# The output product of a mixture kernel as one fp32r product over 96 rows, with the combine weights turned in the last block

## The chip, the cores and the metric

The kernel runs on one core of a Trainium2 chip. The metric is device time in microseconds of one execution; three executions of the kernel before took 632.43, 634.65 and 635.01, median 634.65.

## The reference, cut to what matters

Chunked attention gives x (3072 tokens x 512). A rational feed-forward network follows, and then a soft mixture of 8 experts with 4 slots each, 32 slots in all:

```python
# x: 3072 x 512 from attention
h = x @ w_in                       # 512 x 2048
g = P(h) / (Q(h) + 1e-6)           # a cubic over a quadratic, by element
x = g @ w_out                      # 2048 x 512
logits = x @ phi                   # 3072 x 32
d = softmax(logits, over tokens)   # dispatch
slot_input = d.T @ x               # 32 x 512
for e in range(8):                 # 4 slots per expert
    slot_out[e] = relu(slot_input[e] @ w1[e]) @ w2[e]   # 512x1024, 1024x512
c = softmax(logits, over slots)    # combine
out = c @ slot_out                 # 3072 x 32 times 32 x 512
```

## The kernel before, in words

Tokens are worked in six blocks of 512. A block has eight steps; a step makes 256 hidden features h (24 fp32r products per step, L309: high and low parts of both operands), evaluates the rational function on ScalarE, VectorE and GpSimd, adds to the logits (L326) and turns the result to token order (L334, evicted by L335). The order is written by hand in `KN`: attention of the next block is sliced between the steps; the last block has none and uses `KN['ordl']`. `run_step` issues one part of a step; step kk makes the h of step kk + 1 and finishes the element work of step kk - 1.

After a block, in steps 1 and 2 of the next one, `soft1`, `soft2` and `soft3` work on its logits. `soft2` makes the combine weights `ce`, unnormalised: 128 token rows x 4 x 32 slots. `soft3` adds the dispatched tokens (L387), and ends with a turn of `ce` (L396) into `c_all`, where four groups of 32 partitions hold the 32 slots of four token groups.

Behind the loop: the sums are multiplied by w_out (L605), spread to the experts (L613, L617), then by w1 (L625, in two halves `eq` of four experts), passed through relu, turned (L642) and multiplied by w2 (L652). The result is summed over its four partition groups by a product with `stack` (L658) and evicted (L660). The output stage is the loop at the end: per block two halves, each two products of 32 rows (L668), one VectorE and one ScalarE eviction that scale by the normaliser (L675, L673), and one store (L676). The half tile comes from a pool of two buffers.

w_out, w1 and w2 make 8 + 32 + 32 loads of 512 KB. `fill` issues them on SyncE in a fixed order (`wants`) into whatever slots come free: each call names a pool and a count, and SyncE waits there until the slot's last reader is done. Which slots are named, and where, is the prefetch plan. The first calls stand at step `last` (40), two more `win` slots follow in each step of the last block, and the rest stand between the products behind the loop.

Of the kernel before, what the change touches and what calls it, by code (L numbers as in the profile page):

```python
# [10 lines left out]
F32 = mybir.dt.float32  # L11
F32R = mybir.dt.float32r
AF = mybir.ActivationFunctionType
ALU = mybir.AluOpType
# [27 lines left out]
def tile_chunk_attention__rational__soft_moe(  # L42
# [15 lines left out]
    PE, ACT, DVE, POOL, SP = nc.tensor, nc.scalar, nc.vector, nc.gpsimd, nc.sync  # L58

    NPAIR, P, HP, _ = qw.shape  # L60
    NMEM, D = 8, vwin.shape[-1]
    S = 768
    NT, DM = out.shape
    DFF = 2048
    NSLOT = phi.shape[1]
# [4 lines left out]
    BLK = 512  # L70
    NBLK = NT // BLK
    TT = BLK // P
# [14 lines left out]
    const = Pool(ctx.enter_context(tc.tile_pool(name="const", bufs=1)))  # L87
# [3 lines left out]
    p_S = Pool(ctx.enter_context(tc.tile_pool(name="p_S", bufs=5)))  # L91
    p_g = Pool(ctx.enter_context(tc.tile_pool(name="p_g", bufs=4)))
    p_q = Pool(ctx.enter_context(tc.tile_pool(name="p_q", bufs=1)))
    p_k = Pool(ctx.enter_context(tc.tile_pool(name="p_k", bufs=1)))
    p_v = Pool(ctx.enter_context(tc.tile_pool(name="p_v", bufs=1)))
    p_a4 = Pool(ctx.enter_context(tc.tile_pool(name="p_a4", bufs=2)))
    p_s2 = Pool(ctx.enter_context(tc.tile_pool(name="p_s2", bufs=1)))
    p_dr = Pool(ctx.enter_context(tc.tile_pool(name="p_dr", bufs=1, space=bass.MemoryType.DRAM)))
    p_sm = Pool(ctx.enter_context(tc.tile_pool(name="p_sm", bufs=1)))
# [4 lines left out]
    def bank(shape):  # L104
        return ps_m("m", shape)
# [4 lines left out]
    ident = const("ident", [P, P])  # L110
# [4 lines left out]
    phi_sb = u_acc[:, 0:NC * NSLOT].rearrange("p (c s) -> p c s", c=NC)  # L115
    csum = const("csum", [P, NTILE])
    run = const("run", [P, 4])
    c_all = const("call", [P, NBLK, P])

    ahead = {}  # L120

# [111 lines left out]
    def attention_block(b):  # L233
        new_xt(b)
        for n in range(BLK // (2 * P)):
            yield from attention(b * BLK // (2 * P) + n)
# [77 lines left out]
    st = {}  # L314
# [51 lines left out]
    def soft2(b):  # L366
        pl = st.pop("pl")
        pb = bank([P, TT, 64])
        for tt in range(TT):
            PE.transpose(pb[:, tt, :], pl[0:64, tt * P:tt * P + P], ident[0:64, 0:64])  # L370
        p_tok = p_sm("ptok", [P, TT, NSLOT])
        ACT.activation(p_tok, pb[:, :, 0:32], AF.Copy)  # L372
        cm = p_sm("cm", [P, TT])
        ce = p_sm("ce", [P, TT, NSLOT])
        DVE.tensor_reduce(cm, pb[:, :, 32:64], AX.X, ALU.max)
        DVE.tensor_tensor(ce, pb[:, :, 32:64], cm.unsqueeze(2).to_broadcast([P, TT, NSLOT]), ALU.subtract)
        ACT.activation(ce, ce, AF.Exp)
        DVE.tensor_reduce(csum[:, b * TT:b * TT + TT], ce, AX.X, ALU.add)
        st["ptok"], st["ce"] = p_tok, ce

    def soft3(b):
        ce = st.pop("ce")
        p_tok = st.pop("ptok")
        pb = bank([P, BLK])
        for tt in range(TT):
            for j in range(4):
                PE.matmul(pb[32 * j:32 * j + 32, :], lhsT=p_tok[:, tt, :], rhs=gts[b, j][:, tt, :],  # L387
                          start=(tt == 0), stop=(tt == TT - 1))
        if b == 0:
            DVE.tensor_copy(u_acc, pb)  # L390
        else:
            DVE.scalar_tensor_tensor(u_acc, u_acc, alpha, pb, ALU.mult, ALU.add)
        for j in range(4):
            del gts[b, j]
        pb = bank([P, P])
        PE.transpose(pb, ce.rearrange("p t s -> p (t s)"), ident)  # L396
        ACT.activation(c_all[:, b, :], pb, AF.Copy)

    def wp_chunk(i):
        t = wo.pop(i)  # L400
# [51 lines left out]
    total = NBLK * NSTEP  # L452
# [21 lines left out]
    def fill(pool, tag, count, views):  # L474
        for _ in range(count):
            t = pool(tag, [P, views * 1024])
            for m in range(views):
                if not wants:
                    return
                want = wants.pop()  # L480
                dst = t[:, 1024 * m:1024 * m + 1024]
                if want[0] == "1":
                    src = w1[want[1], want[2] * P:want[2] * P + P, :]
                else:
                    dst = dst.rearrange("p (j d) -> p j d", j=2)
                    src = wo_dr[want[1]] if want[0] == "o" else w2[want[1], want[2]]
                SP.dma_start(out=dst, in_=src)
                got[want] = dst

    def w_out_rows(ft):  # L490
        return got["o", ft // 2][:, ft % 2, :]

    last = total - NSTEP
# [75 lines left out]
    for kk in range(total + 4):  # L569
        b, i = divmod(kk, NSTEP)  # L570
        if kk == last:
            fill(p_q, "q", 1, 1)
            fill(p_a4, "a4", 2, 1)
            fill(p_k, "k", 1, 2)
            fill(p_v, "v", 1, 2)
            fill(p_xt, "xt", 2, 2)
        if i == 0 and b < NBLK - 1:
            state["att"] = attention_block(b + 1)
        for what in KN["ord0" if b == 0 else "ord" if b < NBLK - 1 else "ordl"]:
            run_step(kk, what)  # L580
        if last <= kk < total:
            fill(p_win, "win", 2, 1)
        if kk == total - 1:
            fill(p_xt, "xt", 2, 2)
        if kk == total + 2:
            fill(p_T, "T", 5, 1)
            fill(p_S, "S", 5, 1)
# [8 lines left out]
    pb = bank([P, 4, P])  # L596
# [4 lines left out]
    pb = bank([P, DM])  # L601
    for n in range(4):
        for j in range(4):
            ft = 4 * j + n
            PE.matmul(pb[32 * j:32 * j + 32, :], lhsT=ut[:, n, 32 * j:32 * j + 32],  # L605
                      rhs=w_out_rows(ft),
                      start=(n == 0), stop=(n == 3))
    fill(p_v, "v", 1, 2)
    si = p_s2("s2", [P, DM])
    ACT.activation(si, pb, AF.Copy, scale=rden)  # L610
    pb = bank([P, NC, NSLOT])
# [3 lines left out]
    POOL.memset(sz, 0.0)  # L615
    for e in range(NE):
        DVE.tensor_copy(sz[:, :, e, 4 * e:4 * e + 4], pb[:, :, 4 * e:4 * e + 4])  # L617
    hts = []
    for eq in range(2):
        hb = ps_h("h", [P, 2, 512])  # L620
        for c in range(NC):
            for hh in range(2):
                for j in range(4):
                    e = 4 * eq + j
                    PE.matmul(hb[32 * j:32 * j + 32, hh, :], lhsT=sz[:, c, e, :],  # L625
                              rhs=got[("1", e, c)][:, 512 * hh:512 * hh + 512], start=(c == 0), stop=(c == NC - 1))
        if eq == 0:
            fill(p_win, "win", 12, 1)
        else:
            fill(p_win, "win", 4, 1)  # L630
            fill(p_T, "T", 5, 1)
        h1 = p_a4("a4", [P, 2, 512])
        for hh in range(2):
            if hh:
                ACT.activation(h1[:, hh, :], hb[:, hh, :], AF.Relu)
            else:
                DVE.tensor_scalar(h1[:, hh, :], hb[:, hh, :], 0.0, None, ALU.max)
        hT = (p_k if eq else p_q)("k" if eq else "q", [P, 8, P])
        for hh in range(2):
            pb = bank([P, 4, P])  # L640
            for n in range(4):
                PE.transpose(pb[:, n, :], h1[:, hh, n * P:n * P + P], ident)  # L642
            if hh:
                ACT.activation(hT[:, 4:8, :], pb, AF.Copy)
            else:
                DVE.tensor_copy(hT[:, 0:4, :], pb)
        hts.append(hT)
    so = ps_l("lg", [P, DM])
    for eq in range(2):
        for n in range(8):  # L650
            for j in range(4):
                PE.matmul(so[32 * j:32 * j + 32, :], lhsT=hts[eq][:, n, 32 * j:32 * j + 32],  # L652
                          rhs=got[("2", 4 * eq + j, n // 2)][:, n % 2, :],
                          start=(eq == 0 and n == 0), stop=(eq == 1 and n == 7))
    sos = p_s2("s2", [P, DM])
    ACT.activation(sos, so, AF.Copy)
    pb = bank([P, DM])
    PE.matmul(pb, lhsT=stack, rhs=sos, start=True, stop=True)  # L658
    so4 = p_s2("s2", [P, DM])
    ACT.activation(so4, pb, AF.Copy)  # L660
    rows = out.rearrange("(b r t) d -> b r t d", r=P, t=TT)
    for b in range(NBLK):
        ob = p_xt("xt", [P, TT, DM])
        for half in range(2):
            pb = ps_h("h", [P, 2, DM])
            for m in range(2):
                g = 32 * (2 * half + m)
                PE.matmul(pb[:, m, :], lhsT=c_all[g:g + 32, b, :], rhs=so4[g:g + 32, :], start=True, stop=True)  # L668
            for m in range(2):
                tt = 2 * half + m  # L670
                cs = csum[:, TT * b + tt:TT * b + tt + 1]
                if m:
                    ACT.activation(ob[:, tt, :], pb[:, m, :], AF.Copy, scale=cs)  # L673
                else:
                    DVE.tensor_scalar(ob[:, tt, :], pb[:, m, :], cs, None, ALU.mult)  # L675
            SP.dma_start(out=rows[b, :, 2 * half:2 * half + 2, :], in_=ob[:, 2 * half:2 * half + 2, :])  # L676
# [60 lines left out]
```

## Time and profile before

| what | us |
|---|---|
| median of three executions | 634.65 |
| profiled execution | 633.84 |
| its span | 632.1 |
| TensorE busy | 561.1 |
| VectorE busy | 461.8 |
| ScalarE busy | 421.4 |
| GpSimd busy | 123.5 |

The span is what the trace covers; the profiled execution's own time lies a little over it. Busy shares are means over stages with different limits, so the end of each stage is read from the chain of waits.

### The profile page before, as it was taken

Reading aid. Unit: us, or ns where it says so; the run is one execution under the profiler, and the core shown is the slowest. Engines: PE = TensorE matmul, PEld = TensorE weight load, DVE = VectorE, ACT = ScalarE, POOL = GpSimd, SP = SyncE. Lnnn points to the kernel's source line nnn. Section 1 sums busy time; section 2 is a strip of 40 time slices with the busy share of each in tenths; the row PEclk is TensorE's granted clock in tenths of the full one; section 3 lists DMA queues with packets and bytes.
Section 4 is the critical chain, followed back from the end, with each engine's and each line's share of the span. In section 5 each row is a group of like instructions: output and inputs, shape, how many; then the busy total and the mean of one; then the engine's idle time right before and its main releaser. Section 6 shows DMA issues by size and latency. Waiting matters only on the chain.

```text
span 632.1 us, 13355 instructions
## 1 busy us (share of the span) xinstructions
PE 561.1 (89%) x5784; PEld 377.0 (60%) x5784; DVE 461.8 (73%) x578; ACT 421.4 (67%) x542; POOL 123.5 (20%) x74
## 2 busy tenths in 40 slices
PE   1349999999999999999999999999999997489965
PEld 1338886767666776667765667656776574235211
DVE  3775799977997869978699786997877957620022
ACT  2576899988775878758777586776869688310022
POOL 0121122321231312313133131322223322000000
PEclk9999999999999999999999999999999999689985
DMA  7996745320212202121022210321175236779936
GB/s 308 414 369 218 314 150 200 108 94 1 102 69 90 78 2 101 68 102 67 3 100 68 99 50 21 101 68 63 53 270 184 70 131 226 298 282 409 405 143 266
DMA packets 21754, 97.39 MB, mean 154 GB/s; under 512 B 3136, under 2 KB 3136, under 8 KB 16704
## 3 DMA queue, kind: packets, MB, share of 16 engines
q1 hardware_dynamic: 18000, 79.70, 33.6%
q0 software_dynamic: 2880, 16.78, 7.2%
q8 instruction: 45, 0.74, 0.5%
q10 hardware_dynamic: 816, 0.07, 0.1%
q14 instruction: 13, 0.11, 0.1%
HBM read 86.05 MB, written 10.49 MB: 153 GB/s over the span
## 4 chain that ended last, share of the span: by engine, by line
PE 56%; DVE 18%; ACT 12%; issue 6%; DMA 6%; POOL 1%; DVEq 0%; POOLq 0%; ACTq 0%; SPq 0%
PE h L309 28%; PE lg L326 6%; PE m L334 5%; PE m L387 4%; DMA g<-in_moe_w_in_dram 3%; DVE T L540 3%; DVE T L541 2%; DVE T L555 2%; PE h L625 2%; ACT S L528 2%; ACT g L335 2%; DVE S L529 2%; ACT T L530 2%; DVE T L556 2%; PE h L668 2%
## 5 line engine op out<-in xcount | busy, mean ns | idle before, releaser
L309 PE MATMUL h<-xt,win 128*128 128x512 f32 x1152 | 291.1, 401 | 1.2 <-DVE T L541 0.8
L309 PEld LDWEIGHTS h<-xt,win 128*128 128x128 f32 x1152 | 209.6, 189 | 46.7 <-DVE T L541 1.3
L504 POOL TENSOR_TENSOR S<-S,S 128x1024 f32<-128x1024 f32 x46 | 110.7, 2407 | 315.8 <-DVE S L529 291.0
L529 DVE SCALAR_TENSOR_TENSOR S<-S,S 128x1024 f32<-128x1024 f32 (+1 forms) x49 | 58.8, 1200 | 51.3 <-ACT S L528 51.3
L527 ACT ACTIVATE S<-h,ctab 128x1024 f32<-128x1024 f32 (+1 forms) x49 | 53.7, 1097 | 58.0 <-PE h L309 56.1
L334 PEld LDWEIGHTS m<-ident,T 128*128 128x128 f32 x384 | 42.1, 143 | 46.2 <-issue 22.6
L335 ACT ACTIVATE g<-m 128x512 f32<-128x512 f32 x96 | 55.6, 603 | 18.1 <-PE m L334 18.1
L540 DVE TENSOR_TENSOR T<-T,h 128x1024 f32<-128x1024 f32 (+1 forms) x49 | 58.2, 1188 | 7.6 <-ACT T L530 7.6
L541 DVE SCALAR_TENSOR_TENSOR T<-T,ctab,h 128x1024 f32<-128x1024 f32 (+1 forms) x49 | 61.5, 1254 | 1.3 <-DVE T L540 0.4
L326 PE MATMUL lg<-T,wp 128*32 128x512 f32 x192 | 54.0, 620 | 9.0 <-DVE T L556 9.0
L555 DVE SCALAR_TENSOR_TENSOR T<-T,ctab,S 128x1024 f32<-128x1024 f32 (+1 forms) x49 | 61.3, 1252 | 0.1
L334 PE MATMUL m<-ident,T 128*128 128x128 f32 x384 | 58.2, 285 | 2.3 <-DVE a L182 1.2
L556 DVE SCALAR_TENSOR_TENSOR T<-S,T 128x1024 f32<-128x1024 f32 (+1 forms) x49 | 58.7, 1199 | 1.8
L530 ACT ACTIVATE T<-h,ctab 128x1024 f32<-128x1024 f32 (+1 forms) x49 | 58.9, 1201 | 0.0
L547 ACT ACTIVATE S<-S,ctab 128x1024 f32<-128x1024 f32 (+1 forms) x49 | 55.9, 1144 | 0.6
L546 ACT ACTIVATE S<-S 128x1024 f32<-128x1024 f32 (+1 forms) x49 | 51.5, 1053 | 5.8 <-DVE S L529 3.2
L528 ACT ACTIVATE S<-h,ctab 128x1024 f32<-128x1024 f32 (+1 forms) x49 | 53.7, 1095 | 0.9 <-DVE T L555 0.9
L675 DVE TENSOR_SCALAR xt<-h,csum 128x512 f32<-128x512 f32 x12 | 8.5, 746 | 30.8 <-PE h L668 30.8
L387 PE MATMUL m<-g,ptok 128*32 128x512 f32 x192 | 23.5, 634 | 0.4 <-ACT ptok L372 0.4
L183 ACT ACTIVATE a<-a 128x512 f32<-128x512 f32 x22 | 14.0, 638 | 14.1 <-DVE a L182 14.1
L230 DVE TENSOR_TENSOR xt<-m,xt 128x512 fp32r<-128x512 f32 x24 | 16.5, 688 | 8.5 <-ACT xt L229 8.5
L268 ACT ACTIVATE g<-g 128x1024 uint32<-128x1024 uint32 x16 | 18.5, 1156 | 5.3 <-DMA g<-in_moe_w_in_dram 4.1
(155 smaller groups left out, 614.3 us busy)
## 6 DMA issues: line engine op xcount, KB each, us to landing
win<-in_moe_w_dram SPq DMA_DIRECT2D x32, 512.0 KB, 5.1
k<-in_kw_dram SPq DMA_DIRECT2D x11, 1024.0 KB, 7.4
v<-in_vw_dram SPq DMA_DIRECT2D x11, 1024.0 KB, 4.8
g<-in_moe_w_in_dram POOLq DMA_DIRECT2D x6, 1024.0 KB, 7.3
g<-in_moe_w_out_dram POOLq DMA_DIRECT2D x6, 1024.0 KB, 9.1
out_dram<-xt SPq DMA_DIRECT2D x12, 512.0 KB, 3.2
q<-in_qw_dram SPq DMA_DIRECT2D x11, 512.0 KB, 3.8
T<-in_moe_w_dram SPq DMA_DIRECT2D x10, 512.0 KB, 10.0
```

The costliest lines, as they stand in the source:

```text
L309: PE.matmul(tile_[:, f2, :], lhsT=ww[:, c, f2 * P:f2 * P + P], rhs=xx[:, c, :], start=(n == 0), stop=(n == 3 * NC - 1))
L326: PE.matmul(st["lg"][32 * j:32 * j + 32, :], lhsT=wp[:, 2 * i + f2, :], rhs=t_[:, f2, :], start=(qd == 0), stop=(qd == NF // 4 - 1))
L334: PE.transpose(pb[:, m, f2 * P:f2 * P + P], t_[:, f2, tt * P:tt * P + P], ident)
L335: ACT.activation(gts[b, qd][:, 2 * part:2 * part + 2, 2 * P * o:2 * P * o + 2 * P], pb, AF.Copy)
L504: (POOL if k < total - 2 else DVE).tensor_tensor(out[:, o], q[:, o], w[:, o], ALU.mult)
L528: ACT.activation(y[:, o], hh[:, o], AF.Square, scale=rb1)
L529: DVE.scalar_tensor_tensor(s[:, o], y[:, o], QC, s[:, o], ALU.add, ALU.add)
L530: ACT.activation(t[:, o], hh[:, o], AF.Identity, bias=a2, scale=a3)
L540: DVE.tensor_tensor(t[:, o], t[:, o], hh[:, o], ALU.mult)
L541: behind[kk] = DVE.scalar_tensor_tensor(t[:, o], t[:, o], a1, hh[:, o], ALU.add, ALU.mult).ins
L555: DVE.scalar_tensor_tensor(t[:, o], t[:, o], a0, w[:, o], ALU.add, ALU.mult)
L556: DVE.scalar_tensor_tensor(t[:, o], e[:, o], 2.0, t[:, o], ALU.subtract, ALU.mult, reverse0=True)
```

## The change

The combine weights stay in token order (`c_tok`). A new function `combine_rows(b)` makes three column groups of them for a block: the fp32r rounding of the weights, what that rounding leaves, and the rounding again; it turns them to 96 rows x 512 tokens (`chl[b]`). It is called in steps 3 to 7 of the last block for blocks 0 to 4, and between the w1 products for block 5. The slot outputs are evicted to 96 rows as well (`shl`): rounding, rounding, remainder. One fp32r product over 96 rows then gives high x high + low x high + high x low. Four of the tiles `chl` lie in the k slot and two in the q slot, which therefore take no prefetched weights; the hidden activations of both halves move to the v slot; five S slots are filled after the second half of w1.

```diff
--- before.py
+++ after.py
@@ -115,7 +115,7 @@
     phi_sb = u_acc[:, 0:NC * NSLOT].rearrange("p (c s) -> p c s", c=NC)
     csum = const("csum", [P, NTILE])
     run = const("run", [P, 4])
-    c_all = const("call", [P, NBLK, P])
+    c_tok = const("ctok", [P, NBLK * TT, NSLOT])
 
     ahead = {}
 
@@ -371,15 +371,14 @@
         p_tok = p_sm("ptok", [P, TT, NSLOT])
         ACT.activation(p_tok, pb[:, :, 0:32], AF.Copy)
         cm = p_sm("cm", [P, TT])
-        ce = p_sm("ce", [P, TT, NSLOT])
+        ce = c_tok[:, b * TT:b * TT + TT, :]
         DVE.tensor_reduce(cm, pb[:, :, 32:64], AX.X, ALU.max)
         DVE.tensor_tensor(ce, pb[:, :, 32:64], cm.unsqueeze(2).to_broadcast([P, TT, NSLOT]), ALU.subtract)
         ACT.activation(ce, ce, AF.Exp)
         DVE.tensor_reduce(csum[:, b * TT:b * TT + TT], ce, AX.X, ALU.add)
-        st["ptok"], st["ce"] = p_tok, ce
+        st["ptok"] = p_tok
 
     def soft3(b):
-        ce = st.pop("ce")
         p_tok = st.pop("ptok")
         pb = bank([P, BLK])
         for tt in range(TT):
@@ -392,9 +391,23 @@
             DVE.scalar_tensor_tensor(u_acc, u_acc, alpha, pb, ALU.mult, ALU.add)
         for j in range(4):
             del gts[b, j]
-        pb = bank([P, P])
-        PE.transpose(pb, ce.rearrange("p t s -> p (t s)"), ident)
-        ACT.activation(c_all[:, b, :], pb, AF.Copy)
+    K3 = 3 * NSLOT
+    chl = []
+
+    def combine_rows(b):
+
+        if b % 4 == 0:
+            t = (p_q if b else p_k)("q" if b else "k", [P, 2 if b else 4, BLK], F32R)
+            chl.extend(t[:, n, :] for n in range(2 if b else 4))
+        c3 = p_s2("s2", [P, TT, P], F32R)[:, :, 0:K3].rearrange("p t (k s) -> p t k s", k=3)
+        ce = c_tok[:, b * TT:b * TT + TT, :]
+        for n in (0, 2):
+            ACT.activation(c3[:, :, n, :], ce, AF.Copy)
+        DVE.tensor_tensor(c3[:, :, 1, :], ce, c3[:, :, 0, :].bitcast(F32), ALU.subtract)
+        pb = bank([P, TT, P])
+        for tt in range(TT):
+            PE.transpose(pb[0:K3, tt, :], c3[:, tt].bitcast(F32).rearrange("p k s -> p (k s)"), ident)
+        ACT.activation(chl[b][0:K3, :], pb[0:K3].rearrange("p t r -> p (t r)"), AF.Copy)
 
     def wp_chunk(i):
         t = wo.pop(i)
@@ -569,9 +582,7 @@
     for kk in range(total + 4):
         b, i = divmod(kk, NSTEP)
         if kk == last:
-            fill(p_q, "q", 1, 1)
             fill(p_a4, "a4", 2, 1)
-            fill(p_k, "k", 1, 2)
             fill(p_v, "v", 1, 2)
             fill(p_xt, "xt", 2, 2)
         if i == 0 and b < NBLK - 1:
@@ -582,6 +593,8 @@
             fill(p_win, "win", 2, 1)
         if kk == total - 1:
             fill(p_xt, "xt", 2, 2)
+        if last + 2 < kk < total:
+            combine_rows(kk - last - 3)
         if kk == total + 2:
             fill(p_T, "T", 5, 1)
             fill(p_S, "S", 5, 1)
@@ -605,7 +618,6 @@
             PE.matmul(pb[32 * j:32 * j + 32, :], lhsT=ut[:, n, 32 * j:32 * j + 32],
                       rhs=w_out_rows(ft),
                       start=(n == 0), stop=(n == 3))
-    fill(p_v, "v", 1, 2)
     si = p_s2("s2", [P, DM])
     ACT.activation(si, pb, AF.Copy, scale=rden)
     pb = bank([P, NC, NSLOT])
@@ -615,7 +627,8 @@
     POOL.memset(sz, 0.0)
     for e in range(NE):
         DVE.tensor_copy(sz[:, :, e, 4 * e:4 * e + 4], pb[:, :, 4 * e:4 * e + 4])
-    hts = []
+    combine_rows(NBLK - 1)
+    hts = p_v("v", [P, 2, 8, P])
     for eq in range(2):
         hb = ps_h("h", [P, 2, 512])
         for c in range(NC):
@@ -629,13 +642,14 @@
         else:
             fill(p_win, "win", 4, 1)
             fill(p_T, "T", 5, 1)
+            fill(p_S, "S", 5, 1)
         h1 = p_a4("a4", [P, 2, 512])
         for hh in range(2):
             if hh:
                 ACT.activation(h1[:, hh, :], hb[:, hh, :], AF.Relu)
             else:
                 DVE.tensor_scalar(h1[:, hh, :], hb[:, hh, :], 0.0, None, ALU.max)
-        hT = (p_k if eq else p_q)("k" if eq else "q", [P, 8, P])
+        hT = hts[:, eq]
         for hh in range(2):
             pb = bank([P, 4, P])
             for n in range(4):
@@ -644,28 +658,29 @@
                 ACT.activation(hT[:, 4:8, :], pb, AF.Copy)
             else:
                 DVE.tensor_copy(hT[:, 0:4, :], pb)
-        hts.append(hT)
     so = ps_l("lg", [P, DM])
     for eq in range(2):
         for n in range(8):
             for j in range(4):
-                PE.matmul(so[32 * j:32 * j + 32, :], lhsT=hts[eq][:, n, 32 * j:32 * j + 32],
+                PE.matmul(so[32 * j:32 * j + 32, :], lhsT=hts[:, eq, n, 32 * j:32 * j + 32],
                           rhs=got[("2", 4 * eq + j, n // 2)][:, n % 2, :],
                           start=(eq == 0 and n == 0), stop=(eq == 1 and n == 7))
     sos = p_s2("s2", [P, DM])
     ACT.activation(sos, so, AF.Copy)
     pb = bank([P, DM])
     PE.matmul(pb, lhsT=stack, rhs=sos, start=True, stop=True)
-    so4 = p_s2("s2", [P, DM])
-    ACT.activation(so4, pb, AF.Copy)
+    shl = p_a4("a4", [P, 2, DM], F32R)[:, 0, :]
+    ACT.activation(shl[0:K3, :], pb[0:K3, :], AF.Copy)
+    top = slice(2 * NSLOT, K3)
+    DVE.tensor_tensor(shl[top, :], pb[top, :], shl[top, :].bitcast(F32), ALU.subtract)
     rows = out.rearrange("(b r t) d -> b r t d", r=P, t=TT)
     for b in range(NBLK):
         ob = p_xt("xt", [P, TT, DM])
         for half in range(2):
             pb = ps_h("h", [P, 2, DM])
             for m in range(2):
-                g = 32 * (2 * half + m)
-                PE.matmul(pb[:, m, :], lhsT=c_all[g:g + 32, b, :], rhs=so4[g:g + 32, :], start=True, stop=True)
+                o = (2 * half + m) * P
+                PE.matmul(pb[:, m, :], lhsT=chl[b][0:K3, o:o + P], rhs=shl[0:K3, :], start=True, stop=True)
             for m in range(2):
                 tt = 2 * half + m
                 cs = csum[:, TT * b + tt:TT * b + tt + 1]
```

TensorE, the last block, before: logits and turns of one step, then the h products of the next step but one (`lg`, `m`, `h` are accumulators, `T` the step's result, `xt` tokens, `win` weights).

```order
L326 MATMUL lg_5352<-T_5235,wp_106 32x512 x2
L334 MATMUL m_5429<-ident_103,T_5235 128x128 x4
L334 MATMUL m_5435<-ident_103,T_5235 128x128 x4
L309 MATMUL h_5452<-xt_4230,win_1255 128x512 x4
L309 MATMUL h_5452<-xt_4231,win_1255 128x512 x4
```

The same place on TensorE in the change; `s_12` holds the three column groups of block 1.

```order
L326 MATMUL lg_5327<-T_5214,wp_106 32x512 x2
L334 MATMUL m_5415<-ident_103,T_5214 128x128 x4
L334 MATMUL m_5421<-ident_103,T_5214 128x128 x4
L409 MATMUL m_5435<-ident_103,s_12_5431 96x128 x4
L309 MATMUL h_5448<-xt_4218,win_1255 128x512 x4
L309 MATMUL h_5448<-xt_4219,win_1255 128x512 x4
```

Four turns of 96 columns stand between the step's turns and the h products. ScalarE in the same step of the change (before, rows L410 and L405 are not there):

```order
L540 ACTIVATE S_5441<-h_5379,ctab_105 128x1024
L335 ACTIVATE g_5414<-m_5415 128x2x256
L335 ACTIVATE g_5414<-m_5421 128x2x256
L410 ACTIVATE k_5361<-m_5435 96x512
L541 ACTIVATE S_5443<-h_5379,ctab_105 128x1024
L543 ACTIVATE T_5442<-h_5379,ctab_105 128x1024
L405 ACTIVATE s_13_5499<-ctok_110 128x4x32 x2
L559 ACTIVATE S_5466<-S_5441 128x1024
```

One eviction came between the turns' evictions and L541, and two copies for the next block's rows between L543 and L559. The end of the loads on SyncE, before (`T` slots, then the first stores):

```order
L487 DMA T_5891<-in_moe_w_dram 128x1024
L487 DMA T_5893<-in_moe_w_dram 128x1024
L487 DMA T_5895<-in_moe_w_dram 128x1024
L487 DMA T_5897<-in_moe_w_dram 128x1024
L676 DMA out_dram<-xt_5986 128x1024 x2
```

And in the change:

```order
L500 DMA T_5927<-in_moe_w_dram 128x1024
L500 DMA S_5929<-in_moe_w_dram 128x1024
L500 DMA S_5931<-in_moe_w_dram 128x1024
L500 DMA S_5933<-in_moe_w_dram 128x1024
L500 DMA S_5935<-in_moe_w_dram 128x1024
L500 DMA S_5937<-in_moe_w_dram 128x1024
L691 DMA out_dram<-xt_6026 128x1024 x2
```

Five loads into S slots stand behind the T loads. Ahead of them the first `win` slot to be filled behind the loop is released on TensorE by the row of `win_5136` below, and the next by the row behind the turns:

```order
L638 MATMUL h_5806<-win_5211,a_36_5785 32x512
L638 MATMUL h_5806<-win_5136,a_36_5785 32x512
L409 MATMUL m_5799<-ident_103,s_20_5795 96x128 x4
L638 MATMUL h_5806<-win_5138,a_36_5785 32x512
L638 MATMUL h_5806<-win_5209,a_36_5785 32x512
```

Before, the first released one was `win_5157`, by the eighth product of that line; here it is the fifth.

## Rows read from the trace of the kernel before

**Rows 1.** Chain of waits, 494 to 560 us: start us, us, what.
```profile
502.91 0.26 PE m L396
...
522.20 0.98 PE lg L326 x4
523.18 1.02 PE m L334 x8
524.21 5.47 PE h L309 x24
...
531.29 1.08 ACT g L335 x2
```

**Rows 2.** Timeline of ScalarE, 512 to 530 us: start us, us, instruction, idle before.
```profile
514.97 1.12 ACT L527 ACTIVATE S<-h,ctab 128x1024 f32<-128x1024 f32 x1 [0.31 <-POOL S L504]
516.33 1.09 ACT L335 ACTIVATE g<-m 128x512 f32<-128x512 f32 x2 [0.24 <-PE m L334]
...
519.71 1.07 ACT L546 ACTIVATE S<-S 128x1024 f32<-128x1024 f32 x1 [0.20 <-DVE S L529]
...
522.30 1.11 ACT L527 ACTIVATE S<-h,ctab 128x1024 f32<-128x1024 f32 x1 [0.34 <-POOL S L504]
```

**Rows 3.** Stretches: busy us per engine, PEclk, transfers' share, GB/s.
```profile
556.00:560.60 4.60, 3.91 (x25) 1.12 (x17) 0.75 (x1) 0.28 (x1) 0.00 (x0) 0.80 0.08 19
560.60:600.80 40.20, 36.88 (x301) 16.53 (x300) 3.52 (x12) 3.67 (x6) 0.95 (x1) 0.96 1.01 401
...
612.70:631.00 18.30, 10.78 (x32) 3.87 (x32) 5.64 (x8) 5.83 (x9) 0.00 (x0) 0.50 0.75 299
```

**Rows 4.** Timeline of the SyncE queue, 555 to 633 us: loads and stores.
```profile
559.07 3.81 SPq L487 DMA_DIRECT2D g<-in_moe_w_dram  x8
565.10 1.27 SPq L487 DMA_DIRECT2D v<-in_moe_w_dram  x2
570.95 15.31 SPq L487 DMA_DIRECT2D win<-in_moe_w_dram  x16
587.21 5.46 SPq L487 DMA_DIRECT2D T<-in_moe_w_dram  x5
609.81 18.41 SPq L676 DMA_DIRECT2D out_dram<-xt  x12
```

**Rows 5.** Chain of waits, 600 to 633 us.
```profile
592.34 10.36 DMA T<-in_moe_w_dram
...
602.74 1.92 PE lg L652 x10
...
607.14 1.15 PE h L668 x8
...
608.32 0.76 DVE xt L675
...
609.10 0.69 ACT xt L673
...
609.84 1.15 PE h L668 x4
...
612.54 2.10 PE h L668 x6
...
616.19 2.10 PE h L668 x6
```

**Rows 6.** Groups by line, 493 to 528.8 us: xcount | busy, mean ns of one.
```profile
L309 PE MATMUL h<-xt,win 128*128 128x512 f32 x99 | 24.5, 397 | 0.0
...
L359 DVE COPY s<-m 32x512 f32<-32x512 f32 x1 | 0.7, 683 | 0.0
...
L376 DVE TENSOR_TENSOR ce<-m,cm 128x128 f32<-128x128 f32 x1 | 0.3, 286 | 0.0
...
L372 ACT ACTIVATE ptok<-m 128x128 f32<-128x128 f32 x1 | 0.3, 277 | 0.2 <-PE m L370 0.2
```

**Rows 7.** Page, part 6: KB each and median us from issue to landing.
```profile
out_dram<-xt SPq DMA_DIRECT2D x12, 512.0 KB, 3.2
```

## The prediction

> **What bounds the kernel now.** The edits touch the last block of the loop, the expert stage and the output stage. I read the chain of waits of these three first, then the timeline of the engine that stands closest to it, then the stretches with the share of transfers, and the queue that issues them.
>
> In the last block (to 530 us) the chain is TensorE alone. One step is 0.98 us of logits, 1.02 us of eight turns and 5.47 us of 24 h products, 7.47 us in all, and one piece begins where the other ends [rows 1]. ScalarE is nearly as full. From one Abs at 514.97 to the next at 522.30 it has three short waits, 0.24, 0.20 and 0.34 us, so it works 6.55 of 7.33 us [rows 2]. From 531 to 543 us the tail of the last step alternates between ScalarE and VectorE, while TensorE has little to do.
>
> The expert stage is bound by transfers. From 560.6 to 600.8 us their mean busy share is 1.01 at 401 GB/s, and for 4.6 us before that it is 0.08 [rows 3]. What runs there is the queue's 8 + 2 + 16 + 5 = 31 loads of 0.524 MB [rows 4], 16.25 MB, so one costs 0.524/0.401 = 1.31 us. The chain shows who waits: it lies on the last loads for 10.36 us, and the product behind them ends at 604.66 [rows 5].
>
> The output stage (607.14 to the end) repeats: product 2.10, VectorE 0.76, ScalarE 0.69, next product [rows 5]. Two halves share one such round, because the half tile has two buffers. A round is 609.84 to 612.54 = 2.70 us at first, and 612.54 to 616.19 = 3.65 us later, when the granted clock is 0.50 (1.2 GHz) [rows 3, 5]. Transfers are busy only 0.75 of that time [rows 3].
>
> **Last block.** Rows 0 to 4 of the combine weights are now built in the last block: each is two ScalarE copies, one VectorE subtraction, four turns and one ScalarE eviction. By the order, the turns of the first three stand ahead of h products, so they lengthen a chain of TensorE alone: 4 x 1.02/8 = 0.51 each, 1.53 us. What stands behind such a turn on TensorE is 24 h products, and the step's element work waits for those. The turn itself waits for the subtraction; the copies and the subtraction stand a step earlier in their queues, so I expect no wait there. The other two come in the last step, beside idle TensorE. There the eviction of one (512 wide, like half of the 1.08 us pair of L335 [rows 1], say 0.55) stands ahead of L528 on the chain, and one subtraction (0.29, as L376 [rows 6]) ahead of L556: 0.84 us. Against that, six turns of L396 go. The chain has 0.26 for one [rows 1], a turn in a stream is 0.13, and five of them lie in busy TensorE: 0.65 back. Sum +1.7. Lower end +0.2: the copies hide, the removed turns count 0.26 each and the added ones save idle slots. Upper end +4, the first rival.
>
> ScalarE gets 0.55 + 2 x 0.28 (L372 [rows 6]) = 1.1 us per step. That makes 6.55 + 1.1 = 7.65 of a step that grows to 7.98, which is why I count only TensorE.
>
> **Loads.** The old plan sends 41 loads before the g slots, the new one 38: the q and k slots now hold the turned weights and take none. The v slot, now the hidden activations, no longer takes two loads, and five S loads are added at the end. So the saturated stretch carries 8 + 16 + 5 + 5 = 34 loads in place of 31: 3 x 1.31 = +3.9 us. Nothing covers this, since the matmuls behind the last loads already wait for them [rows 5]. The lost v loads also filled time: eight g loads are through at about 560.6 + 8 x 1.31 = 571.1, and the first win load was issued at 570.95 [rows 4], waiting for a product to release it. In the new order that release is a few matmuls earlier, but four turns of row 5 stand between. A load alone lands 3.2 us after issue [rows 7], 1.9 more than its transfer, so a hole of 0 to 1.9 us; I take 0.6. Bounds of the whole term: 0, if these loads never decide, and +6.
>
> The Trainium skill, "DMA: Bandwidth & Descriptors", section "Specifications", gives about 358 GB/s from HBM for a core. That stretch holds 401 [rows 3], so the trace does not bear it out. By the page's figure an estimate for three loads is 4.4 us, and the output stage below would gain about 2 us in place of 4.2.
>
> **Head of the output.** So far two ScalarE evictions with one product between. Now the second evicts 96 rows, and a VectorE subtraction on 32 rows x 512 follows before the first output product. L359, 32x512, is 0.68 [rows 6]; with its start +0.75. Ends 0.3 (as L376) and 1.0.
>
> **Output.** Twelve halves, each two fp32r products of 96 rows instead of two fp32 products of 32 rows, which lie side by side. The trace has no fp32r product of 96 rows. The nearest is L309, 128 rows, 24 in 5.47 us = 0.23 each, one alone 0.40 [rows 1, 6]: half = 0.23 + 0.40 = 0.63 at full clock, about 1.1 at 1.2 GHz. Upper end 2.1, as now; lower end 0.4. A round becomes 0.63 + 0.09 + 0.76 + 0.69 = 2.2, or 2.65 at the low clock. Six rounds and one more eviction (0.7) put the last store at 13.9 to 16.6 us after the start; now it is 20.7. As the span ends 4.2 us after the last store's issue [rows 4], engines alone would end at 18.1 to 20.8. But the stores need the transfer time: the first is issued after 2.2, lands 3.2 later [rows 7], eleven more at 1.31 follow, 1.0 to the end: 2.2 + 3.2 + 14.4 + 1.0 = 20.8. Now it is 632.1 - 607.14 = 24.95. So -4.2, and from here on the transfers end last, not the round. Ends -3 (rounds of 2.9) and -6.8 (stores that cost nothing).
>
> The Trainium skill, "TensorE: Matmul & The Clock Gate", section "Part 3: Packing small matmuls — row/col tiling", speaks against this edit: products of 32 rows in different row strips run at the same time, so packing is the gain to keep. The trace agrees on the old pair (eight records in 1.15 us [rows 5]). An estimate by the rule alone would let each half grow by one product, 0.23 us, twelve times 2.8; that is inside the 0.63 above and beneath the stores.
>
> **Sum.** 1.7 + 3.9 + 0.6 + 0.75 - 4.2 = +2.8 us. The profiled execution took 633.84 (span 632.1 and 1.7 around it), 0.8 under the median of three, 634.65. So 636.6 for such an execution, 637.4 for the median. A measurement here tells 0.5% (3.2 us) from no change: under 631.5 is faster, over 637.8 slower.
>
> **Rivals.**
> First, slower: ScalarE becomes the bound of the last block. For it: the eviction of L410 stands ahead of L541, which starts the loop ScalarE, VectorE, GpSimd and back to the next Abs, and the 0.34 us wait for GpSimd ends that loop in each step [rows 2]. If none of its waits shrink, a step is 7.33 + 1.1 = 8.4, not 7.98, and the two copies also fall into the last step's chain: 3 x 0.45 + 0.56 + about 0.4 of turns waiting = +2.3, 639.7. It decides where the loop's length passes 7.98. Against it: those waits sum to 0.78, and most end when TensorE lets them.
> Second, not slower: the three loads do not decide. For it: the 4.6 us before 560.6 with almost no transfers [rows 3], which earlier releases could fill, and the product's matmuls, which could be the longer chain. Then 3.9 + 0.6 go: 632.9, and with the lower end of the last block 631.4. Against it: the share of 1.01 for 40 us, and the release that ends the empty stretch is not moved ahead.
> Third: the change does not do what it says at the output. Rounds stay near 3 us because the low clock doubles the products and evictions keep their order; the gain is 3, so 638.6.
>
> **Chances.** Forecast 0.48, first 0.22, second 0.22, third 0.08. Of the forecast, whose own range is 635.5 to 639.3, a little under half lies above 637.8; nearly all of the first and most of the third; of the second, under half lies below 631.5. Together: faster 0.10, same 0.43, slower 0.47. The range 632.4 to 640.6 takes in the second rival's time and the first's with an upper end of the loads, and leaves 2 in 10.
>
> **What would show it.** The last block: steps of 8.0 us on TensorE with L409 between L334 and L309; if they are 8.4 with ScalarE waits of zero, the first rival holds. Loads: 34 from the g slots on, share near 1 to the end, a hole of half a microsecond before the first win load, the product ending 6 us later in the span than 604.66. If the product's end moves by under 3 us, the second holds. Output: rounds of 2.2 to 2.7, transfers busy at about 1, 20.8 us from first product to the end; rounds of 3 and a share below 0.9 mean the third. I am wrong altogether if the time falls below 631: then some part of the load stretch was not a bound at all.

## The result, and the profile after

The changed kernel takes 639.41 us (median of 6 runs, 637.22 to 640.45), the kernel before 633.92 beside it (6 runs, 632.43 to 635.01): a ratio of 1.0085, 95% interval 1.006 to 1.0109, so 5.5 us slower where 2.8 were forecast. The profiled execution took 638.15, its span is 636.0.

Where the span went, by marks that both traces have (step n is the start of VectorE's L541, now L554, in step n of the loop; u is the first eviction behind the long product L387, now L386):

| stretch | before | after | difference | forecast |
|---|---|---|---|---|
| start to step 0 | 69.48 | 68.09 | -1.39 | 0 |
| step 0 to 43 | 431.27 | 430.91 | -0.36 | +1.7 for these |
| step 43 to 47 (last block) | 36.46 | 38.24 | +1.78 | three stretches, |
| step 47 to u (its tail) | 22.00 | 22.36 | +0.36 | -0.65 included |
| u to the end of the last w2 product | 45.43 | 51.83 | +6.40 | +4.5 |
| head of the output | 2.50 | 3.27 | +0.77 | +0.75 |
| output | 24.93 | 21.33 | -3.60 | -4.2 |

The start is earlier by chance: in the traces of these two and of the ten kernels below, which all do the same work up to step 0, step 0 lies between 68.09 and 69.76, in no order that goes with an edit. Without it the spans differ by 5.4 us, which agrees with the medians.

**Last block.** The chain of waits of the kernel after, where [rows 1] had three pieces to a step:

```profile
521.31 0.98 PE lg L326 x4
522.29 1.02 PE m L334 x8
523.32 0.44 PE m L409 x4
523.75 5.48 PE h L309 x24
...
531.93 0.48 ACT k L410
...
541.38 1.06 PE m L409 x4
...
554.60 4.98 PE m L386 x32
```

TensorE is still without a gap; four turns, 0.44 us together, stand in each of three steps, which are 7.92 long instead of 7.47. The eviction L410 has joined the chain of the last step (0.48), and one set of turns stands in the tail at a granted clock of 0.50 (1.06).

The timeline of VectorE, and that of GpSimd, in the same step (start us, us, instruction):

```profile
518.74 1.22 DVE L553 TENSOR_TENSOR T<-T,h 128x1024 f32<-128x1024 f32 x1
519.87 1.66 DVE L406 TENSOR_TENSOR s<-ctok,s 128x128 fp32r<-128x128 f32 x1
521.45 1.27 DVE L554 SCALAR_TENSOR_TENSOR T<-T,ctab,h 128x1024 f32<-128x1024 f32 x1
```
```profile
518.97 2.41 POOL L517 TENSOR_TENSOR S<-S,S 128x1024 f32<-128x1024 f32 x1 [5.35 <-DVE S L542]
```

The subtraction of 128x128 lasts 1.66 us here, though the same line lasts 0.28 where GpSimd is idle: it ends at 521.53, just behind the end of GpSimd's L517 (518.97 + 2.41 = 521.38). This happens in three steps.

**Loads.** The stretches that answer to [rows 3] (PEclk, the transfers' share and GB/s are the last three columns), then the queue that answers to [rows 4]:

```profile
556.00:560.60 4.60, 3.64 (x30) 0.88 (x23) 1.12 (x3) 0.00 (x0) 0.00 (x0) 0.88 0.24 70
560.60:608.00 47.40, 42.18 (x308) 12.60 (x307) 3.70 (x13) 4.78 (x9) 0.95 (x1) 1.00 0.97 376
571.00:577.00 6.00, 5.34 (x52) 1.43 (x44) 0.56 (x1) 0.00 (x0) 0.00 (x0) 1.00 0.92 287
578.00:586.00 8.00, 7.57 (x68) 2.13 (x60) 0.85 (x2) 0.60 (x1) 0.00 (x0) 1.00 1.02 413
617.00:634.00 17.00, 10.37 (x20) 5.08 (x20) 7.74 (x11) 7.66 (x12) 0.00 (x0) 0.50 0.89 357
```
```profile
559.47 3.94 SPq L500 DMA_DIRECT2D g<-in_moe_w_dram  x8
569.65 17.28 SPq L500 DMA_DIRECT2D win<-in_moe_w_dram  x16
587.88 5.45 SPq L500 DMA_DIRECT2D T<-in_moe_w_dram  x5
594.28 5.45 SPq L500 DMA_DIRECT2D S<-in_moe_w_dram  x5
617.13 15.17 SPq L691 DMA_DIRECT2D out_dram<-xt  x12
```

The 34 loads are there. From 571 to 577 they ran at 287 GB/s instead of some 410: 6 x (1 - 287/410) = 1.8 us of transfer time are missing, three times the hole that was forecast. It lies behind the issue of the first win load (569.65) and not ahead of it. The 16 win loads took 17.28 us to issue instead of 15.31. The chain of waits in that place has row 5's turns between the products, and a win load as what the next products wait for:

```profile
567.72 1.90 PE h L638 x10
569.62 0.57 PE m L409 x4
570.19 1.01 PE h L638 x7
571.20 6.14 DMA win<-in_moe_w_dram
```

**Head and output.** The chain of waits that answers to [rows 5]:

```profile
599.41 10.08 DMA S<-in_moe_w_dram
...
609.53 1.92 PE lg L665 x10
...
613.96 0.70 DVE a L675
...
614.70 0.90 PE h L683 x2
...
617.16 1.24 PE h L683 x2
...
618.42 0.76 DVE xt L690
...
619.20 0.70 ACT xt L688
...
619.94 1.24 PE h L683 x2
```

The last loads still lie on the chain. A round is 617.16 to 619.94 = 2.78 us, and the next ones are as long; before, it was 3.65 at the same clock of 0.50. The product fell from 2.10 to 1.24, and nothing else in the round changed. The stores' share of the transfers is 0.89.

### The profile page after: what moved, and what is told of

Read it like the earlier page. It is cut to its first block, busy times and chain, and to the rows that moved or that the text cites. A ratio compares the mean times of both kernels' runs of the same rounds, so it can differ in the third digit from the quotient of the medians.

```text
span 636.0 us, 13379 instructions
## 1 busy us (share of the span) xinstructions
PE 566.2 (89%) x5778; PEld 375.2 (59%) x5778; DVE 468.1 (74%) x585; ACT 426.2 (67%) x554; POOL 123.5 (19%) x74
## 4 chain that ended last, share of the span: by engine, by line
PE 54%; DVE 18%; ACT 12%; DMA 8%; issue 7%; POOL 1%; ACTq 0%; POOLq 0%; DVEq 0%; SPq 0%
PE h L309 28%; PE lg L326 6%; PE m L334 5%; PE m L386 4%; DMA win<-in_moe_w_dram 3%; DVE T L553 3%; DMA g<-in_moe_w_in_dram 2%; DVE T L554 2%; DVE T L568 2%; ACT S L541 2%; ACT g L335 2%; DVE S L542 2%; ACT T L543 2%; PE m L426 2%; DMA T<-in_moe_w_dram 2%
## 5 line engine op out<-in xcount | busy, mean ns | idle before, releaser
L517 POOL TENSOR_TENSOR S<-S,S 128x1024 f32<-128x1024 f32 x46 | 110.7, 2407 | 316.7 <-DVE S L542 291.9
L553 DVE TENSOR_TENSOR T<-T,h 128x1024 f32<-128x1024 f32 (+1 forms) x49 | 58.2, 1189 | 7.6 <-ACT T L543 7.6
L554 DVE SCALAR_TENSOR_TENSOR T<-T,ctab,h 128x1024 f32<-128x1024 f32 (+1 forms) x49 | 61.4, 1253 | 1.1 <-DVE T L553 0.4
L543 ACT ACTIVATE T<-h,ctab 128x1024 f32<-128x1024 f32 (+1 forms) x49 | 58.8, 1200 | 0.0
L559 ACT ACTIVATE S<-S 128x1024 f32<-128x1024 f32 (+1 forms) x49 | 51.4, 1052 | 4.8 <-POOL S L517 2.6
L541 ACT ACTIVATE S<-h,ctab 128x1024 f32<-128x1024 f32 (+1 forms) x49 | 53.6, 1094 | 0.9 <-DVE T L568 0.9
L386 PE MATMUL m<-g,ptok 128*32 128x512 f32 x192 | 23.0, 622 | 0.4 <-ACT ptok L372 0.4
L225 PE MATMUL m<-ident,a 128*128 128x128 f32 x88 | 14.6, 291 | 7.8 <-DVE a L216 6.8
L206 PE MATMUL m<-v,a 64*32 64x64 f32 x1408 | 20.9, 231 | 0.4 <-ACT a L198 0.2
```

Source lines behind the costliest of these rows:

```text
L517: (POOL if k < total - 2 else DVE).tensor_tensor(out[:, o], q[:, o], w[:, o], ALU.mult)
L541: ACT.activation(y[:, o], hh[:, o], AF.Square, scale=rb1)
L543: ACT.activation(t[:, o], hh[:, o], AF.Identity, bias=a2, scale=a3)
L553: DVE.tensor_tensor(t[:, o], t[:, o], hh[:, o], ALU.mult)
L554: behind[kk] = DVE.scalar_tensor_tensor(t[:, o], t[:, o], a1, hh[:, o], ALU.add, ALU.mult).ins
```

## The experiments

All ratios are to the kernel before, run beside it on the same chip, with 95% intervals.

**1. The load plan alone, on the kernel before** (e1)

```
-            fill(p_q, "q", 1, 1)
-            fill(p_k, "k", 1, 2)
...
-    fill(p_v, "v", 1, 2)          # behind the u product
...
             fill(p_T, "T", 5, 1)
+            fill(p_S, "S", 5, 1)
```


> The kernel before with the new load plan alone: no loads into the q and k slots in the last block, none into the v slot after the u product, five S loads at the end; turns, combine weights and output product as before. My theory: the 31 loads from the g slots on become 34 (3 x 1.28 = +3.8 us), and with the v loads gone the transfers run dry for 1 to 2 us before the first win slot is released; the product behind the last loads ends 5 to 6 us later than 604.66 and the time is 1.007 to 1.010 of before (+4.5 to +6). First rival, the hole belongs to the turns of row 5 alone: then +3.8 and no hole (1.006). Second rival, the loads do not decide and the last block does: within 1 us of before.


Measured: 638.54 us, 1.0068 (1.0046 to 1.009). From u to the end of the last w2 product 49.54 us instead of 45.43: +4.1. The stretch at 570 to 576 us:

```profile
570.00:576.00 6.00, 6.00 (x51) 5.22 (x45) 0.00 (x0) 0.00 (x0) 0.00 (x0) 0.83 0.97 373
```

The dip is about half a microsecond, (1 - 373/410) x 6 = 0.5. So the three loads cost what they were priced at, and the lost v loads about the half microsecond that was forecast for the hole: the first rival is the nearest.

**2. All six rows turned behind the w1 products, on the kernel after** (e2)

```
-        if last + 2 < kk < total:
-            combine_rows(kk - last - 3)
...
-    combine_rows(NBLK - 1)        # ahead of the w1 products
...
+    for b in range(NBLK):
+        combine_rows(b)
     so = ps_l("lg", [P, DM])
```


> The kernel after with all six calls of combine_rows moved behind the two rounds of w1 products, where TensorE waits for loads; load plan and output as after. My theory: the last block loses its +1.8 us, and the second win slot is released right behind the first, since no turns stand between, so 1 to 1.5 us of the hole go as well: 2.8 to 3.3 us under after, about 636 against 639.4 (1.004 of before). First rival, the last block's extra time is hidden by what follows: only the hole's 1.3 goes. Second rival, the hole comes from the v loads that are no longer made: only the 1.8 of the block go and the dry stretch from 571 to 577 stays as it was (2 us of transfer time missing). Third, six rows in one place lengthen the expert stage: the last w2 product waits for them and not for loads, and the time is that of after or more.


Measured: 633.9 us, 0.9997 (0.9983 to 1.0012): the whole loss is gone, 5.5 us, though the longer load plan is still in. Steps 43 to 47 are back at 36.44, from u to the last w2 product it takes 49.75 us. The third rival falls: a load is still what the last product waits for, as the chain shows.

```profile
594.34 10.08 DMA S<-in_moe_w_dram
604.46 1.92 PE lg L664 x10
```

That is 2.2 us more than the upper end of what I expected. The tail is the place that I had left out: 20.66 us from step 47 to u, against 22.36. But 1.2 of these 1.7 are its long product (L386), which took 3.76 us here at a granted clock of 1.00 and 4.98 at 0.75 in the kernel after; that the edit did this is not shown.

**3. Row 5 alone moved** (e3): of the edit above only the line of `combine_rows(NBLK - 1)`.


> The kernel after with one call moved: row 5 of the combine weights is turned behind the two rounds of w1 products and not ahead of them; rows 0 to 4 stay in the last block, the load plan is the new one. My theory: the dry stretch of the transfers at 571 to 577 belongs to these four turns, since the next win slots wait for the products behind them; with them gone the transfers run at 400 GB/s throughout, the w1 stage is 1.3 us shorter and the w2 stage 0.8: about 2.1 us under after, 1.005 of before. The other 3.4 us that moving all six rows gave are the last block's. Rival: the turns fall into waits for loads anyway, the whole gain of moving all six was the last block's and the granted clock's: within 0.5 us of after (1.008).


Measured: 639.98 us, 1.0098 (1.0079 to 1.0117): no gain that four runs show. From u to the last w2 product it takes 50.54 us, 1.3 less than in the kernel after; but the same long product of the tail took 6.60 us and that of u 5.38 where the kernel after had 4.98 and 3.69. The chain, the stretch of the long product with a later one, and the queue:

```profile
555.73 6.60 PE m L386 x32
...
564.56 5.38 PE m L618 x32
```
```profile
555.70:562.30 6.60, 6.46 (x32) 1.39 (x32) 1.35 (x5) 0.31 (x1) 0.00 (x0) 0.56 0.29 114
574.00:576.00 2.00, 2.00 (x24) 1.87 (x20) 0.00 (x0) 0.00 (x0) 0.00 (x0) 1.00 0.54 115
```
```profile
562.21 3.76 SPq L500 DMA_DIRECT2D g<-in_moe_w_dram  x8
574.09 14.23 SPq L500 DMA_DIRECT2D win<-in_moe_w_dram  x16
```

The granted clock was 0.56 in the long product. Up to the u product this kernel's code is that of the kernel after, so this is one execution against another, and not the edit. The longer u product also opened a gap of its own: the first win load is issued 11.88 us behind the first g load, where the kernel after has 10.18, and from 574 to 576 us the transfers ran at 115 GB/s, so that (1 - 115/410) x 2 = 1.4 us are missing again. The timed runs miss my 1.005 too; they have no traces, and I can't show that they lost it in the same way.

**4. Rows 0 to 4 alone moved** (e11): row 5 stays ahead of the w1 products (row slots taken in the order k, q).


> The kernel after with rows 0 to 4 of the combine weights turned behind the two rounds of w1 products; row 5 stays ahead of the first w1 products, and the load plan is the new one: the other half of the split of which moving row 5 alone was the first. My theory: the steps 43 to 47 lose their 1.80 us, the tail behind them the turns and the eviction of row 4 on its chain (1.06 + 0.48 + 0.2, less what the granted clock of its long product does, which has stood at 3.8 to 6.6 us between executions), the loads keep their dry stretch: 3 to 3.8 us under after, 1.003 to 1.004 of before. Rival: row 5's move gained nothing by itself because the granted clock took back what the loads gave; then nearly all of the 5.5 us that moving six rows gave is here, and the time is that of before (1.000).


Measured: 635.55 us, 1.0039 (1.0023 to 1.0055), as the theory had it: against the kernel after, 0.0046 of before, or 2.9 us, belong to rows 0 to 4 in the last block. The dry stretch stayed:

```profile
570.00:576.00 6.00, 5.15 (x51) 1.55 (x43) 0.69 (x1) 0.38 (x1) 0.00 (x0) 1.00 0.84 305
```

Against e2, which differs by row 5 alone, it is slower by 0.0042, some 2.7 us; the intervals don't touch. So moving row 5 is worth something when the other rows are out of the last block, and nothing could be measured when they are in it. In the same way rows 0 to 4 cost 2.9 us with row 5 in its place and 6.4 with it moved (e3 against e2, 0.0101): the two moves don't simply add.

**5. The output product with the old load plan** (e4): e2's edit, the turned rows in three S slots, the q, k and v loads back, no S loads at the end.

```
-            t = (p_q if b else p_k)("q" if b else "k", [P, 2 if b else 4, BLK], F32R)
+            t = p_S("S", [P, 2, BLK], F32R)
...
+            fill(p_q, "q", 1, 1)
+            fill(p_k, "k", 1, 2)
```


> The fp32r output product with the load plan of before: the turned weights of the six rows lie in three S slots, which come free behind the w1 products, and are built there; q, k and v slots take their loads again, the S slots none at the end. My theory: the extra loads, the hole and the last block's turns cost all of the loss, so with them gone only the head (+0.8), the output (-3.65) and the removed turns (-0.4 and some of the last block) are left: 3.2 to 3.8 us under before, 0.994 to 0.995. Rival: the rows' work in the expert stage (six times 1.5 to 2 us of TensorE waiting for ScalarE and VectorE) ends later than the last loads and gives back 3 to 5 us: the time is that of before or slower, with the last w2 products waiting for the rows and not for a transfer.


Measured: 630.52 us, 0.9942 (0.9921 to 0.9962), as the theory had it. From u to the last w2 product 45.62 us, as before; the rows' work is hidden behind the loads.

**6. Half of each store left out, on the kernel after** (e6): `rows[b, :, 2 * half:2 * half + 1, :]` and the same half of `ob`; the other half of the output is not written.


> The kernel after with every store cut to the first of its two token tiles, so that half of the output is not written; products and evictions as after. My theory: the rounds of product, VectorE and ScalarE (2.78 us for two halves) set the output stage, and the stores wait for them: the rounds stay at 2.7 to 2.8, only the last store's landing is shorter, 0.5 to 1 us under after. Rival, which is the forecast's own step: the transfers end last; then 12 x 0.65 = 8 us of transfers go, and the stage is 3 us or more shorter, down to what the rounds allow.


One execution, 637.43 us. The chain of its output stage, and the transfers' share in it:

```profile
620.86 1.24 PE h L683 x2
...
622.12 0.76 DVE xt L690
...
622.91 0.69 ACT xt L688
...
623.65 1.24 PE h L683 x2
```
```profile
618.00:632.00 14.00, 10.38 (x20) 5.19 (x20) 7.36 (x10) 6.80 (x11) 0.00 (x0) 0.50 0.49 188
```

With half the bytes the rounds are still 2.79 us (620.86 to 623.65), so they bind and not the stores. The stage takes 19.51 us, 1.8 less: a store of VectorE's tile alone doesn't wait for ScalarE's eviction (0.7), the first product took 0.74 instead of 0.90, and the last store lands sooner.

**7. The evictions side by side.** In both kernels one half of the output is one PSUM tile of two banks, and ScalarE's eviction of the second bank waits for VectorE's of the first, as the chain shows in each round. Four runs give each product a tile of its own: the kernel before with three banks in turn (e8) and with four (e10), the fp32r product with the old plan with four (e9), and the kernel after with four (e5). The edit of e10 (in e8 both tiles come from the three banks of `ps_m`):

```
-            pb = ps_h("h", [P, 2, DM])
+            pb = [ps_m("m", [P, DM]) if half else ps_h("h", [P, DM]) for _ in range(2)]
             for m in range(2):
...
-                PE.matmul(pb[:, m, :], lhsT=c_all[g:g + 32, b, :], rhs=so4[g:g + 32, :], start=True, stop=True)
+                PE.matmul(pb[m], lhsT=c_all[g:g + 32, b, :], rhs=so4[g:g + 32, :], start=True, stop=True)
```


> The kernel before with each half of the output put into two PSUM tiles of one bank in place of one tile of two banks; the fp32 product, the load plan and everything else as before. In both kernels the ScalarE eviction of a half starts only when the VectorE eviction of the same tile has ended. My theory: the rounds bind the output stage of before, not the product as such, so with the evictions side by side a half takes 1.05 at the low clock and the stores take over at 1.31 each: output 24.95 to about 20.5 us, the time 4 to 4.5 us under before (0.993). Rival, TensorE binds: the product of a half at the low clock and the wait for the third bank give rounds near 3.4: under 1.5 us gained. Second rival: the evictions side by side gain their 0.7 per round and no more, 6 x 0.7 = 4, which differs from the first only in the share of transfers, below 0.9.

> The kernel before (fp32 output product on 32 rows) with each half of the output in two PSUM tiles of one bank, four in turn: the two products of a half can lie side by side as before, which three banks did not allow, and the evictions too. My theory: TensorE needs 1.05 us a half at the low clock, the stores 1.3, so the stores take over: output 24.95 to 20.5, the time 4 to 4.5 us under before (0.993), without fp32r, without the turned rows and without the new plan. Rival: at the low clock the fp32 products are the bound, whatever the banks: rounds of 3.4 or more for two halves, at most 1.5 us gained.

> The fp32r output product with the load plan of before (rows in S slots, built behind the w1 products), and each half of the output in two PSUM tiles of one bank, four in turn, so that the ScalarE eviction of a half doesn't wait for the VectorE one. My theory: the first store is issued 0.7 us sooner, products at the low clock take 1.24 a half and stores 1.28 to 1.31, so that now the transfers end last: output 21.6 to about 19.8 us, the time 1.5 to 2 us under the version with one tile a half (630.5), 0.991 of before. Rival: the stores bound the stage already, then only the first store's 0.7 us.

> The kernel after with each half of the output in two PSUM tiles of one bank, four in turn, so that the ScalarE eviction doesn't wait for the VectorE one; plan and rows as after. My theory: the rounds bind, not the stores, so the stores close up to 1.28 us each and the stage goes from 21.3 to 19.7 us: 1.5 us under after, 1.006 of before. Rival: the time of the stores was the bound: no more than the first store's 0.7 us.


Measured: e8 634.99 us, 1.0018 (1.0001 to 1.0035); e10 628.66, 0.9926 (0.9909 to 0.9943); e9 630.15, 0.9947 (0.9926 to 0.9967); e5 637.36, 1.0064 (1.0044 to 1.0084). The chain of e8 first, then the stretch of e10's stores:

```profile
609.45 5.57 PE m L668 x12
615.03 0.04 issue
615.06 5.72 PE m L668 x12
```
```profile
608.70:625.00 16.30, 12.25 (x40) 4.41 (x40) 7.66 (x11) 7.10 (x11) 0.00 (x0) 0.58 0.95 379
```

With three banks three products take 2.9 us (612.15 to 615.06), where four took 2.73 before: two start 0.1 us apart and the third 0.7 later, and each next one starts as an eviction frees its bank. TensorE is on the chain nearly throughout, and the stage grew from 24.93 to 26.8 us. My theory for e8 was wrong and its first rival the nearest. With four banks the pair stays together, the share of the transfers rises from 0.75 to 0.95, and the stage takes 20.27 us. e10 has the lowest ratio of all kernels run, with the fp32 product, the old plan and no turned rows, though its interval overlaps those of e4 and e9: no run shows that the fp32r product is worth anything beside this edit. In e5 the queue shows the stores issued faster than in the kernel after (13.00 us for twelve instead of 15.17), and the stage takes 19.73 us instead of 21.33. The ratio is 0.0021 lower, as expected, though the two intervals overlap:

```profile
616.62 13.00 SPq L691 DMA_DIRECT2D out_dram<-xt  x12
```

In e9's trace the output stage takes 19.73 us instead of 21.64 in e4, but the times of these two can't be told apart, so the 0.991 that I expected was missed. In the two profiled executions the tail took 1.7 us more in e9 (22.35 against 20.66), with its long product at another granted clock (0.69 and 1.00).

## Why the prediction was right, and where its terms were off

- The time lies in the range, 2.0 us over the forecast; slower was right. But the difference was 5.5 us and not 2.8, and 639.41 lies just above the forecast's own range (635.5 to 639.3): that the whole range held it is owed to the room that it left for the first rival, whose mechanism did not come. By the table 1.9 of the 2.7 us too many are in the loads' stretch and 0.6 in the output. e1 and e4 bear out the loads and the output with its head; e11 puts rows 0 to 4 at 2.9 us, where 1.53 + 0.84 = 2.4 were counted.
- **Loads** (+3.9): +4.1 by e1, right. **Head** (+0.75): +0.77, right.
- **The hole** (0.6): too small. The lost v loads make 0.5 of it (e1); what was not priced is the four turns of row 5 between the products that release the first win slots. In the four traces with these turns the second win load is issued 1.55 us behind the first, in the three with 34 loads and no turns there 0.43. Between u and the last w2 product the four take 50.39 to 51.90 us and the three 49.54 to 50.54. Compared at the same length of the u product, the turns cost 1.3 on average at 3.69 us (after, e5, e11 against e1, e2) and 1.4 at 5.38 (e6 against e3); in the profiled execution it was 2.2. The 3.2 us of [rows 7] that the hole was worked out from is the landing of a store; before, the first g load landed 3.45 us after its issue, so that this changes little.
- **Last block** (+1.7): the steps were well priced (turns 0.44 where 0.51 was taken, eviction 0.48 where 0.55 was), and in the profiled pair the whole term is right, +1.78, but partly by luck: the long product of the tail took 4.98 us there and 5.46 before. What was left out is the tail. I took the turns of the last step to lie "beside idle TensorE"; row 4's stand ahead of the logits and lie on the chain with 1.06 us. The tail is 22.36 to 23.90 in the four traces with rows there and 20.66 to 22.35 in eight without: 1.4 on average. Of that, 0.8 is the long product at other granted clocks (5.8 us on average against 5.0), which no run ties to the rows; 0.65 is left for the turns and the rest of the row. The five turns of L396 in busy TensorE gave 0.36, not 0.65.
- **Output** (-4.2): this step fails in its reason. "From here on the transfers end last, not the round" is not so: e6 took half the bytes away and the rounds stayed, e5 and e10 took the wait between the evictions away and the stage became shorter. That is the third rival's mechanism, by its own marks: 2.78 us a round, a share of 0.89. It cost 0.6 us against the forecast; the two limits lie close, since two stores at 1.31 need 2.62. I had seen in [rows 5] that ScalarE follows VectorE, and counted both one behind the other, but did not ask whether they had to.
- **The first rival** gave 639.7, next to the measured time, and is wrong: steps are 7.92 and not 8.4, and TensorE has no gap in them. ScalarE's waits shrank instead, from 0.78 us between two Abs to 0.45. What I expected of the subtraction, no wait, was wrong (1.66 us), but nothing on TensorE waited for those three.
- **The second rival** (loads do not decide) is refuted by e1 and e4.

Open: why moving row 5 alone gained nothing in time (e3), while moving it as well as the others did (e2 against e11). In e3's trace the turns' 1.4 us are gained and lost again by a u product at a lower granted clock; that the timed runs lost them so is the likeliest reason, but the clock was only seen, not changed.

## What to carry to other kernels

Before an engine in a round is made faster, see whether two others in it run one behind the other for no reason but a shared tile: parting that tile took 4.7 us off the output stage of the kernel before, against 3.6 for the new product in the same place. Behind the new product, whose rounds were shorter, it took off 1.6 in the trace of e5, and the times show no clear gain (e5 and e9). Count the slots that a change takes from a prefetch, since each load that moves into a saturated stretch costs its full transfer time (1.3 us). Work that is added anyway belongs where the engines wait for transfers: the six rows cost 0.2 us there (e2 against e1, u to the last w2 product), and about 5.5 us where they were.

## What the runs showed of the hardware

- A VectorE subtraction of 128x128 with both inputs in SBUF lasted 0.28 us alone and 1.64 to 1.66 us beside a GpSimd multiplication, until 0.15 us behind its end, in all twelve cases of four traces (after, e3, e5, e6); L553, which has one input in PSUM, kept its 1.22 us beside the same GpSimd instruction. The Trainium skill, "SBUF — State Buffer", section "Who interferes with whom", says that a VectorE instruction with two SBUF inputs contends with a GpSimd one that reads SBUF, since its second input comes through the read interface that the two share; the traces agree.
- The granted clock of one and the same stretch differs between executions. The long product of the tail (32 records) took 3.76 us at a granted clock of 1.00 (e2, that is 2.4 GHz), 4.98 at 0.75 (after), 5.46 at 0.69 (before), 6.38 at 0.58 (e6) and 6.60 at 0.56 (e3), where a mean below 1.00 says that a part of it ran at 1.2 GHz; after, e3 and e6 run the same code up to there. In the 13 to 14 us ahead of it, in which TensorE was busy for 7.9 to 10.1, the mean was 0.72 to 0.76 in all five.
- Two halves of the output in fp32, each a pair of 32-row products in different row strips, took 2.73 us together at a granted clock of 0.50; the 2.10 of [rows 5] end with the first of the two pairs. The four fp32r products of 96 rows in their place took 2.07. The rows, before and after:

```profile
612.54 2.73 PE L668 MATMUL h<-s,call 32*128 32x512 f32 x8 [0.92 <-ACT xt L673]
617.16 2.07 PE L683 MATMUL h<-a,k 96*128 96x512 f32 x4 [0.71 <-ACT xt L688]
```
